# Split weights in slots 3, 5 and 7 of the first expert mixture, and later rank and list steps in its slots

## The chip, the cores and the metric

The kernel runs on one core of one Trainium2 chip. The metric is device time in microseconds (us) of one execution, taken as the median of several runs. Where the text speaks of a profile, it is one execution recorded by the hardware profiler: for each engine the start and the duration of every instruction. Engines are named as the profile names them: PE is the TensorE matmul, PEld its weight load, DVE is VectorE, ACT is ScalarE, POOL is GpSimd, SP is SyncE, whose queue issues the large DMAs.

## What is computed

Attention over 2 x 8 heads of 576 positions feeds a mixture of 8 experts (capacity 288 tokens each), and its output feeds a second mixture of 8 experts. The change lies in the first mixture:

```python
h = np.maximum(np.einsum('ecd,edf->ecf', disp, w1), 0.0)
y = np.einsum('ecf,efd->ecd', h, w2)
for i in range(N):
    if keep[i]:
        out[i] = gate_w[i] * y[expert_idx[i], pos[i]]
```

Here `disp` holds the tokens of an expert (512 features), `w1` is 512 x 1024 and `w2` 1024 x 512 for each expert, all in 32-bit floats. There are 1152 tokens for 8 experts, so an expert has about 144.

## The kernel before

The kernel works in stages: attention (to 108 us in the profile), eight slots of the first mixture (112 to 269 us), five slots of the second (from 269 us). A slot is one expert with a fixed number of token columns. The widths of slots 0 to 7 are 160, 192, 136, 152, 132, 160, 144 and 168; the fullest experts go to the wide ones.

A slot has eight steps (j = 0 to 7), one for each piece of 1024 weight columns, 512 KB. Steps 0 to 3 form the hidden layer from the tokens `xs`, steps 4 to 7 the output `yT` from `hidden`. Each step makes eight products, one weight block of 128 x 128 times all token columns of the slot, so a slot makes 64 products.

There are two ways to make a product (`product`, L848). A native slot multiplies the 32-bit floats directly (L853): the trace shows two matmul records for each product, each with a weight load. A halved slot splits weights and tokens into a head (`hi`, rounded to a shorter mantissa) and a rest (`lo`), and makes two matmuls: the head of the weight times heads and rests of the tokens side by side (L857, twice the columns), and the rest of the weight times the heads of the tokens (L859, one time the columns). Before the change slot 1 alone is halved (L48).

A halved slot needs more from ACT and DVE. `split` (L747) makes for each half piece a cast on ACT (L757) and a subtraction on DVE (L759), 16 of each in a slot. `prep` (L812) turns the tokens on PE in two halves and writes them by a cast on ACT (L845) and a subtraction on DVE (L846), where a native slot has one copy on ACT (L841). `fold` and `fold2` (L902, L921) empty PSUM by an extra copy on ACT and an addition on DVE, and write `hidden` as head and rest.

The order of the work is written by hand on a clock of the kernel's own: `step` (L865) adds the estimated time of each product. `stream` (L1116) asks for piece i of a slot seven steps ahead (`tf`, L1127), and cuts it five steps ahead (`ts`, L1128), so that the pieces 0 to 4 of a halved slot are cut in steps 3 to 7 of the slot before it, and pieces 5 to 7 in its own steps 0 to 2. Piece buffers (`st`) number eight. A native slot gives a buffer back when PE has used it, a halved slot when the piece is split. SP issues the fetches (L142) in a fixed order, among them each slot's write of its result rows (L1013), and reads a register for the second mixture (L1052) that `choose` (L1223) writes in slot 6. Each slot's tail (`tail1`, L947) runs beside the next slot: the second mixture's gate, the rank matmuls (L984 to L987) at `k.T[3]` and the list matmuls (L1016) at `k.T[4]` or `k.T[6]` on the kernel's clock. `T` asks for ranks at 5.6 and lists at 13.0 or 9.9, `TH` at 6.6, 14.2 and 10.9; slot 0 has `TH`, slots 1 to 6 have `T`, slot 7 has `TL`. The tokens of the next slot are turned from step 6 on (L1206), the second half 2.0 later on that clock.

PE's order is pinned. On ACT and DVE the build chooses an order within the given constraints, and each engine then works through its instructions in that order.

```python
clock[0] += k.c / 600 + 0.005 if k.native else \
    k.c / 800 + 0.005 + (k.c / 10000 + 0.021 if 2 * k.c <= 512 else 0.0)
```

Of the kernel before, what the change touches and what calls it, by code (L numbers as in the profile page):

```python
# [16 lines left out]
N, DM, E, F = 1152, 512, 8, 1024  # L17
# [25 lines left out]
T = 1.5, 2.3, 3.0, 5.6, 9.9, 2.0, 13.0  # L43
TL = 0.9, 1.7, 2.4, 4.6, 9.4, 2.0, 13.0
AWAKE = 15, 6, 14, 4
DW = 128 + 2 * E
MID, PLACE = 32, 1.2
HALVED = 1,  # L48
TH = 1.5, 2.3, 3.0, 6.6, 10.9, 2.0, 14.2
BRISK = 1.2  # L50

# [37 lines left out]
def build(tc, ctx, spots, tab, qk, v, s, wg, wa, cap, mod, wg2, mb, wb, out):  # L89
# [687 lines left out]
    def gather(k, idx, xc=None, rows=None):  # L777
        k.xc = xc or rings[k.m][turn[k.m] % 3]
        turn[k.m] += not xc
        k.idx = idx  # L780
        src, rw = (x1, RW) if k.m == 1 else (y1[0:rows or E * C1, :], RW2)
        for i, (_, r) in enumerate(k.rows):
            nc.gpsimd.indirect_dma_start(  # L783
                out=k.xc[:r, i, 0:rw], out_offset=None, in_=src,
                in_offset=bass.IndirectOffsetOnAxis(ap=idx[:r, i:i + 1], axis=0),
                bounds_check=src.shape[0] - 1, oob_is_err=False)
# [7 lines left out]
    def begin(g):  # L794

        agenda.append([clock[0], clock[0], g])
# [15 lines left out]
    def prep(k, after=None):  # L812
        c = k.c
        k.xs = mp.tile([P, 4, c], F32, tag="xs", name="xn", bufs=1) if k.native else \
            mp.tile([P, 4, 2, c], F32R, name="xs", bufs=1)
        per = 2 if 2 * c <= 512 else 1

        def turn_rows(pt, kp, i):
            r0, r = k.rows[i]
            for kk in range(per):  # L820
                kt = kp + kk
                pin(nc.tensor.transpose(pt[:, kk, r0:r0 + r], k.xc[:r, i, kt * P:(kt + 1) * P], ident[:r, :r]))

        ready = {}
        if after is None and per == 2:
            for i in range(len(k.rows)):
                for kp in (0, 2):
                    if not i:
                        ready[kp] = pt_.tile([P, per, c], F32, tag="t", name="ptx")
                    turn_rows(ready[kp], kp, i)  # L830
        for kp in range(0, 4, per):
            if kp:
                yield (1.0 * kp if after else 0.0)
            pt = ready.get(kp)
            if pt is None:
                pt = pt_.tile([P, per, c], F32, tag="t", name="ptx")
                for i in range(len(k.rows)):
                    turn_rows(pt, kp, i)
            with tc.issue_after(after.relu) if after else ExitStack():
                if k.native:  # L840
                    ins = nc.scalar.copy(k.xs[:, kp:kp + per], pt)  # L841
                    fence(ins)
                    continue
                hi = k.xs[:, kp:kp + per, 0, :]
                ins = nc.scalar.copy(hi, pt)  # L845
            fence(ins, nc.vector.tensor_tensor(k.xs[:, kp:kp + per, 1, :], pt, hi.bitcast(F32), op=ALU.subtract))  # L846
# [208 lines left out]
    def pick(m, lst, cv, n=None):  # L1055
        idx = mp.tile([HC[m], W[m]], I32, name="idx", bufs=4)
        src = lst[:, bass.ds(cv, W[m])]
        if n is None:
            nc.gpsimd.tensor_copy(idx, src)
        else:  # L1060
            nc.gpsimd.tensor_tensor(idx, src, hole[:, n, :], op=ALU.add)
        return idx
# [19 lines left out]
    def slot(m, width=None, halved=False):  # L1082
        k = Slot()
        k.m, k.c, k.two = m, width or C[m], True
        k.native = (m == 1 or k.c == H2) and not halved
        k.rows = [(r, min(HC[m], k.c - r)) for r in range(0, k.c, HC[m])]
        k.ranked = k.placed = k.listed = lambda: None
        k.early, k.T, k.last, k.hold, k.next = False, T, False, None, None
        return k
# [20 lines left out]
    def at(n, j, f):  # L1110
        steps.setdefault(8 * n + j, []).append((8 * n + j - 1, f))
# [4 lines left out]
    def stream(n, k, src, known, pace=0.5, late=()):  # L1116

        k.w, k.st = {}, {}

        def get(i):  # L1120
            with tc.issue_after(k.hold()) if k.hold else ExitStack():
                k.st[i] = first[i] if n == 0 and i < len(first) else fetch(src, k.e, i)

        def cut(i):
            k.w[i] = k.st.pop(i) if k.native else split(k.st.pop(i), i, alone=n < E or i in late)
        for i in range(8):
            tf = max(8 * n + i - FETCH, known + pace * i)  # L1127
            ts = 8 * n + i - 2 if i in late else max(8 * n + i - SPLIT, tf + (2 if n < E else 3))  # L1128
            when(tf, lambda i=i: get(i))
            when(ts, lambda i=i: cut(i))  # L1130
# [55 lines left out]
    def know(k, e):  # L1186
        k.e, k.cv = where(1, perm, e - 1)

    for e in range(E):
        k = slot(1, WID[e], e in HALVED)  # L1190
        if seq:
            seq[-1].next = k
        k.early = e not in (E - 3, E - 1)
        k.T = TL if e == E - 1 else TH if e + 1 in HALVED else T
        k.e = e
        k.tail = lambda k=k, e=e: tail1(k, e)
        stream(e, k, wa, never)
        if e:
            steps.setdefault(8 * e - 8, []).append((never, lambda k=k, e=e: know(k, e)))
            at(e - 1, 1, lambda k=k, e=e: gather(k, pick(1, list1, k.cv, n=e)))  # L1200
        else:
            gather(k, list0)
            tc.keep_in_program_order(nc.gpsimd.tensor_copy(hole, con["hole"][:H1]))
            tc.keep_in_program_order(nc.gpsimd.memset(run, 0.0))
            k.idx = pick(1, list1, 0, n=0)
        at(max(e - 1, 0), 6 if e else 0, lambda k=k, e=e: begin(prep(k, after=seq[e - 1])) if e else list(prep(k)))  # L1206
        seq.append(k)
# [116 lines left out]
    for i in range(5):  # L1324
        n = E + i
        k = slot(2, H2 if i == 4 else C2)
# [97 lines left out]
```

## Time and profile before

| | us |
|---|---|
| median of 3 runs | 406.28 |
| lowest and highest of them | 405.71, 406.42 |
| the profiled execution | 402.02 |
| its span, first to last instruction | 400.2 |
| PE busy in the span | 385.4 |

The profiled execution is a run of its own, 4.3 us below the median. Its span leaves 1.8 us around it. Busy time counts an engine as busy while an instruction runs on it; what ended an idle time stands in brackets in the timeline rows. The granted clock is the share of TensorE's full clock; it is 0.996 over the span.

### The profile page before, as it was taken

To read this page: it belongs to the slowest core of one execution; us is meant where nothing else is said; L and a number is where in the kernel's file an instruction comes from. 1 tells how busy PE (TensorE), PEld (TensorE's weight loads), DVE (VectorE), ACT (ScalarE), POOL (GpSimd) and SP (SyncE) were. 2 spreads that over 40 slices of the span, in tenths; PEclk is the share of its full clock that TensorE was granted. 3 is DMA by queue.
4 is the path that set the end of the run, shared out by engine and by line. 5 is a ranking of instruction groups with operands and counts; after the bars stand their busy time and mean duration, and the time that the engine had idled before them with its cause. 6 is when DMAs were issued, how large, how long until landed. Compare 5 with 4: busy or idle time off the path is not lost. (4 is left out here: it accounts for less than half of the span.)

```text
span 400.2 us, 8788 instructions
## 1 busy us (share of the span) xinstructions
PE 385.4 (96%) x3144; PEld 358.1 (89%) x3144; DVE 194.8 (49%) x781; ACT 179.6 (45%) x471; POOL 133.4 (33%) x177
## 2 busy tenths in 40 slices
PE   6899999999999999999999999999999999999991
PEld 3688888898689899999999999999999999999981
DVE  7977778887726853241415051559822342221100
ACT  7999999986325722121212121245423464131220
POOL 5776977550273311210102004000437266030031
PEclk9999999999999999999999999999999999999998
DMA  5864798702159942978797678971169557010020
GB/s 184 276 197 155 262 380 331 269 3 88 50 150 329 379 136 63 322 203 303 226 310 251 236 224 273 275 253 50 42 165 383 167 160 217 12 34 26 2 55 22
DMA packets 30626, 74.66 MB, mean 187 GB/s; under 512 B 9234, under 2 KB 11666, under 8 KB 30572
## 3 DMA queue, kind: packets, MB, share of 16 engines
q1 hardware_dynamic: 24120, 66.73, 49.7%
q0 software_dynamic: 6368, 7.22, 6.8%
q8 instruction: 27, 0.44, 0.5%
q14 instruction: 27, 0.22, 0.2%
q10 hardware_dynamic: 84, 0.04, 0.0%
HBM read 63.78 MB, written 10.51 MB: 186 GB/s over the span
## 5 line engine op out<-in xcount | busy, mean ns | idle before, releaser
L853 PE MATMUL ps<-xn,st 128*128 128x160 f32 (+6 forms) x512 | 70.4, 290 | 0.4 <-ACT xn L841 0.4
L853 PEld LDWEIGHTS ps<-xn,st 128*128 128x128 f32 x512 | 66.2, 190 | 0.6 <-ACT xn L841 0.6
L853 PE MATMUL ps<-hidden,st 128*128 128x160 f32 (+5 forms) x448 | 62.9, 294 | 0.0
L853 PEld LDWEIGHTS ps<-hidden,st 128*128 128x128 f32 x448 | 58.5, 190 | 0.5
L482 ACT ACTIVATE e<-sc,nmx 128x192 f32<-128x192 f32 (+4 forms) x80 | 44.7, 561 | 3.0 <-DVE sc L478 2.4
L919 DVE COPY yT<-ps 128x276 f32<-128x276 f32 (+6 forms) x22 | 8.0, 362 | 69.2 <-ACT yT L918 69.2
L861 PE MATMUL ps<-xs,hi 128*128 128x276 f32 x128 | 38.4, 300 | 0.0
L861 PE MATMUL ps<-hidden,hi 128*128 128x276 f32 x128 | 38.1, 298 | 0.0
L862 PE MATMUL ps<-xs,hi 128*128 128x276 f32 x128 | 37.1, 290 | 0.0
L863 PE MATMUL ps<-xs,lo 128*128 128x276 f32 x128 | 37.1, 290 | 0.0
L863 PE MATMUL ps<-hidden,lo 128*128 128x276 f32 x128 | 37.1, 290 | 0.0
L862 PE MATMUL ps<-hidden,hi 128*128 128x276 f32 x128 | 37.0, 289 | 0.0
L783 POOL DMA_INDIRECT xc<-x,idx x14 | 15.1, 1078 | 63.2 <-DVE eq L976 46.6
L394 PE MATMUL pt<-ident,e 128*128 128x128 f32 x240 | 34.7, 275 | 0.8 <-ACT eT L498 0.7
L918 ACT COPY yT<-ps 128x276 f32<-128x276 f32 (+6 forms) x22 | 7.1, 323 | 58.6 <-PE ps L853 31.2
L478 DVE TENSOR_SCALAR_CACHE_REDUCE sc<-ps 128x192 f32<-128x192 f32 (+4 forms) x80 | 31.6, 417 | 2.3 <-ACT e L482 0.8
L394 PE MATMUL ps<-ka,qa 128*128 128x320 f32 (+2 forms) x96 | 29.9, 326 | 2.0 <-DVE qa L358 1.3
L759 DVE TENSOR_TENSOR lo<-st,hi 128x512 fp32r<-128x512 f32 x40 | 27.4, 707 | 5.8 <-ACT hi L757 5.7
L1023 POOL DMA_INDIRECT out<-yr,oi x12 | 14.4, 1201 | 45.6 <-ACT yr L940 43.2
L757 ACT CAST hi<-st 128x512 fp32r<-128x512 f32 x48 | 27.6, 619 | 4.5 <-DMA st<-in_wa 4.5
L394 PEld LDWEIGHTS pt<-ident,e 128*128 128x128 f32 x240 | 26.2, 141 | 1.8 <-ACT eT L498 0.9
L932 DVE SCALAR_TENSOR_TENSOR hidden<-ps,hidden 128x552 fp32r<-128x552 f32 x16 | 11.7, 732 | 30.0 <-ACT hidden L930 29.9
(301 smaller groups left out, 854.2 us busy)
## 6 DMA issues: line engine op xcount, KB each, us to landing
st<-in_wa SPq DMA_DIRECT2D x64, 512.0 KB, 5.6
st<-in_wb SPq DMA_DIRECT2D x24, 512.0 KB, 6.4
qkd<-in_qk SPq DMA_DIRECT2D x6, 1152.0 KB, 5.4
y<-yr SPq DMA_DIRECT2D x8, 390.0 KB, 3.8
vt<-in_v SPq DMA_DIRECT2D x8, 320.0 KB
qkd<-in_qk SPq DMA_DIRECT2D x4, 576.0 KB, 4.9
out<-zrow SPq DMA_DIRECT2D x1, 2304.0 KB
x<-xrow SPq DMA_DIRECT2D x2, 768.0 KB
```

Of the source, the lines that this page charges most:

```text
L394: ins = op(*args, **kw)
L478: least[:] = [nc.vector.tensor_scalar(h.sc[t][:r, c0:c1], ps[:r, o0:o0 + c1 - c0], -0.125, low, op0=ALU.mult, op1=ALU.min, accum_out=h.nmx ...
L482: recent[:] = [nc.scalar.activation(ebuf[t, i][:r, :w], h.sc[t][:r, :w], AF.Exp, bias=h.nmx[t][:r], scale=-1.0, accum_out=rsum[:r, k.b, t, ...
L757: nc.scalar.copy(hi[:, c:c + h], st[:, c:c + h])
L759: eng.tensor_tensor(lo[:, c:c + h], st[:, c:c + h], hi[:, c:c + h].bitcast(F32), op=ALU.subtract)
L783: nc.gpsimd.indirect_dma_start(out=k.xc[:r, i, 0:rw], out_offset=None, in_=src, in_offset=bass.IndirectOffsetOnAxis(ap=idx[:r, i:i + 1], a ...
L853: pin(nc.tensor.matmul(out[:, 0:c], w[:, o:o + P], mv, start=first, stop=last, skip_group_check=True))
L861: pin(nc.tensor.matmul(out[:, 0:c], hi, mv[:, 0, :], start=first, stop=False, skip_group_check=True))
L862: pin(nc.tensor.matmul(out[:, 0:c], hi, mv[:, 1, :], start=False, stop=False, skip_group_check=True))
L863: pin(nc.tensor.matmul(out[:, 0:c], lo, mv[:, 0, :], start=False, stop=last, skip_group_check=True))
L932: fence(relu, nc.vector.scalar_tensor_tensor(k.hs[:, 2 * j:2 * j + 2, 1, :], k.b, 0.0, hi.bitcast(F32), op0=ALU.max, op1=ALU.subtract))
L1023: put = nc.gpsimd.indirect_dma_start(out=out, out_offset=bass.IndirectOffsetOnAxis(ap=oi[:, i:i + 1], axis=0), in_=yr[:, i, :], in_offset= ...
```

## The change

The tuple of halved slots grows from slot 1 to slots 1, 3, 5 and 7, and slots 1 to 6 take the later set of times `TH`.

```diff
-HALVED = 1,
+HALVED = 1, 3, 5, 7
 TH = 1.5, 2.3, 3.0, 6.6, 10.9, 2.0, 14.2
...
-        k.T = TL if e == E - 1 else TH if e + 1 in HALVED else T
+        k.T = TL if e == E - 1 else TH
```

By it, slots 3, 5 and 7 (152, 160 and 168 columns) multiply split heads and rests. Slot 7 keeps `TL`.

## Rows read from the trace of the kernel before

**Rows 1.** The page, busy us, share of the span and instructions.
```profile
PE 385.4 (96%) x3144; PEld 358.1 (89%) x3144; DVE 194.8 (49%) x781; ACT 179.6 (45%) x471; POOL 133.4 (33%) x177
```
**Rows 2.** Busy by stretch, slots 0, 1, 3, 5, 7: length; PE, PEld, DVE, ACT, POOL; clock; DMA.
```profile
112.58:130.69 18.11, 18.11 (x137) 18.11 (x137) 8.59 (x17) 8.01 (x18) 8.79 (x15) 1.00 0.84 271
130.69:152.79 22.10, 21.73 (x163) 20.75 (x162) 12.74 (x43) 9.86 (x21) 4.96 (x5) 1.00 0.61 222
170.95:190.71 19.76, 19.76 (x163) 19.01 (x161) 6.01 (x32) 3.88 (x11) 2.15 (x3) 1.00 0.80 260
208.40:228.99 20.59, 20.59 (x162) 19.78 (x161) 6.20 (x32) 3.97 (x11) 2.19 (x3) 1.00 0.75 245
247.41:268.64 21.23, 21.23 (x166) 20.72 (x165) 10.22 (x39) 6.68 (x17) 0.50 (x1) 1.00 0.86 252
```
**Rows 3.** Timeline of PE, native runs: start, length, engine, line, operation, columns, records.
```profile
181.03 4.30 PE L853 MATMUL ps<-hidden,st 128*128 128x152 f32 x32
218.90 4.51 PE L853 MATMUL ps<-hidden,st 128*128 128x160 f32 x32
258.35 2.44 PE L853 MATMUL ps<-hidden,st 128*128 128x168 f32 x16
383.46 1.70 PE L853 MATMUL ps<-xn,st 128*128 128x92 f32 x14
```
**Rows 4.** Timeline of PE and PEld, slot 1 (halved) and a slot of 276 columns.
```profile
142.26 0.36 PE L857 MATMUL ps<-hidden,hi 128*128 128x384 f32 x1
...
146.56 0.36 PE L857 MATMUL ps<-hidden,hi 128*128 128x384 f32 x1
...
131.26 0.19 PEld L857 LDWEIGHTS ps<-xs,hi 128*128 128x128 f32 x1
131.37 0.19 PEld L859 LDWEIGHTS ps<-xs,lo 128*128 128x128 f32 x1
...
367.86 0.29 PE L861 MATMUL ps<-hidden,hi 128*128 128x276 f32 x1
...
369.90 0.29 PE L862 MATMUL ps<-hidden,hi 128*128 128x276 f32 x1
```
**Rows 5.** Timeline of PE, the rank matmul in slot 1; idle time before it in brackets.
```profile
139.75 0.21 PE L984 MATMUL pr<-oh,upper 96*96 96x16 bf16 x1 [0.37 <-DVE oh L981]
```
**Rows 6.** Timeline of ACT and DVE, end of slot 0, before the halved slot 1.
```profile
124.31 1.14 ACT L757 CAST hi<-st 128x512 fp32r<-128x512 f32 x2 [1.29 <-DMA st<-in_wa]
126.86 1.14 ACT L757 CAST hi<-st 128x512 fp32r<-128x512 f32 x2 [0.64 <-DMA st<-in_wa]
128.27 1.14 ACT L757 CAST hi<-st 128x512 fp32r<-128x512 f32 x2
129.31 0.48 ACT L845 CAST xs<-ptx 128x384 fp32r<-128x384 f32 x1
129.19 1.28 DVE L759 TENSOR_TENSOR lo<-st,hi 128x512 fp32r<-128x512 f32 x2
130.39 0.55 DVE L846 TENSOR_TENSOR xs<-ptx,xs 128x384 fp32r<-128x384 f32 x1
```
**Rows 7.** Timeline of SP: third pieces of slots 3, 5, 7, and a fourth piece.
```profile
160.26 0.33 SPq L142 DMA_DIRECT2D st<-in_wa  x1
198.02 0.33 SPq L142 DMA_DIRECT2D st<-in_wa  x1
236.92 0.34 SPq L142 DMA_DIRECT2D st<-in_wa  x1
240.23 0.33 SPq L142 DMA_DIRECT2D st<-in_wa  x1
```
**Rows 8.** Line L142, issue to landing in us, slot 2, then slot 4.
```profile
DMA to landing us min/median/max: 5.5/5.5/5.5
DMA to landing us min/median/max: 6.0/6.0/6.0
```
**Rows 9.** Waits of SP's queue in slot 6: us in total, times, longest.
```profile
SPq L1052 <- DVE sres L1235: 1.7, 1, 1.7
```

## The prediction

> **What bounds the kernel now.** I read the page first: PE is busy for 385.4 of 400.2 us, while DVE and ACT stand below half [rows 1]. Then the stretches by slot: in the native slots 3, 5 and 7 PE is busy for the whole stretch at a granted clock of 1.00, the higher level of 2.4 GHz; slot 1, the halved one, has 0.37 us in which PE is idle [rows 2]. So in these slots the end is set by what PE has to stream, and whatever PE is made to wait for is added in full. A saving on PE counts only while DVE, ACT and the fetches keep up. That is why I then read the price of a product in either form, and after that what surrounds the start of the one halved slot.
>
> **Price of a native product.** 32 records in a run of 4.30 us at 152 columns, less the 0.30 that the last one takes by itself, stand 129.0 ns apart. At 160 columns it is 135.8 ns, at 168 columns 142.0 ns [rows 3]. Two records make a product: 258, 272 and 284 ns.
>
> **Price of a halved product.** At 192 columns fifteen products go by between 142.26 and 146.56, so one costs 286.7 ns [rows 4]. I need it at 152 to 168 columns, which the trace of before doesn't show. Two rows say how it is made up. The load of the head and the load of the rest that follows it start 110 ns apart, 131.26 and 131.37 [rows 4], and native passes of only 92 columns also stand 110 ns apart ((1.70 - 0.27)/13) [rows 3]. So I take 110 ns as the least time between two matmuls that each need a new block of weights. The rest's matmul at 192 columns needs less than that by its columns, so it costs 110 ns, and the head's matmul (384 columns) has what is left, 177 ns or 0.461 ns a column. In a slot of 276 columns sixteen matmuls from 367.86 to 369.90 stand 127.5 ns apart [rows 4], 0.462 ns a column: the same rate. With that, a product costs 110 + 0.461 x 2c: 250 ns at 152 columns, 257.5 at 160, 265 at 168. The saving is 7.9, 14.1 and 19.1 ns a product, 41.1 ns in all, times 64 products: **2.6 us**. It is small because only the head's matmul gets cheaper with fewer columns. The bounds are 2.0 and 3.2 us, from 3 ns a product either way, the difference between the two readings of the rate plus the rounding of the rows.
>
> The Trainium skill, page "TensorE: Matmul & The Clock Gate", section "Back-to-back issue gap", gives about 81 ns for a matmul of 128 columns with its load, less than the 110 taken here. By it the rest's matmul would cost about 25 ns less a product, some 4.8 us more saving in all by an estimate from that page. The 92-column passes at 110 ns speak against it.
>
> **What the halved form adds on PE.** Slot 1 lasts 22.10 us; less 64 x 0.2867 and the 0.37 of waiting, 3.38 us are left for transposes, gate, ranks and lists. Slot 5 has 20.59 - 64 x 0.2716 = 3.21 us for the same [rows 2 to 4]. So 0.17 us a slot, **0.5 us** for three.
>
> **The rank wait.** In slot 1 PE waits 0.37 us for the one-hots of the tail [rows 5], because DVE has the last splits between the steps of that chain. In slots 3, 5 and 7 the chain has the same work beside it; by the kernel's clock the ranks come after 27 to 29 products instead of 24, at 250 to 265 ns instead of 287, so some 0.3 us later in real time. That nearly closes the gap. I take **0.2 us** for three slots; the bounds are 0 and 1.1 (three times 0.37). Asking later for ranks and lists in the other slots costs PE nothing: the same matmuls are made, only a few products later, and the lists are still within the slot. What waits for a list is the gather for slot 8, whose tokens are turned only near the end of slot 7.
>
> **The start of the halved slots.** This is the term that decides. At the end of slot 0 ACT and DVE work in the order in which the code asks: split of piece 2 (124.31), copy of `yT`, split of piece 3, first half of `xs`, split of piece 4, second half of `xs`, whose subtraction ends at 130.39 + 0.55 = 130.94. ACT stood idle for the landing of piece 2 (1.29 us) and of piece 3 (0.64 us) [rows 6]: work behind a piece that isn't there waits with it. From the landing of piece 2 to the second half of `xs` it is 130.94 - 124.31 = 6.6 us, of which 0.64 us is the wait for piece 3; so 6.0 to 6.6 us. Slot 1 started at 130.69 [rows 2] and needed that half for its third product, two products or 0.57 us later: there were 0.3 us to spare.
>
> In slots 2, 4 and 6 piece 2 of the next slot is issued later against the slot's end, since the write of result rows stands in the same queue and the rows of a gather come at the same time. It is issued at 160.26, 198.02 and 236.92 [rows 7]; landing takes 5.5 us in slot 2 and 6.0 in slot 4 [rows 8], and I take 5.75 in slot 6. It is there at 165.8, 204.0 and 242.7. Adding 6.0 to 6.6, the second half of `xs` is written at 171.8 to 172.4, 210.0 to 210.6 and 248.7 to 249.3. PE wants it two products (0.5 us) after the starts at 170.95, 208.40 and 247.41 [rows 2]: 171.45, 208.9, 247.9. So PE waits 0.35 to 0.95, 1.1 to 1.7 and 0.8 to 1.4 us, together 2.3 to 4.0 us; I take **3.1 us**. While the slots were native their `xs` was one copy on ACT with no split ahead of it, so nothing of this wait exists now. What follows it is not late: the splits that come next have their pieces, and the rank chain moves with the slot.
>
> **Other edits.** 24 more pieces are split, 48 casts and 48 subtractions (0.57 and 0.64 us each in pairs [rows 6]), some 10 us of ACT and DVE a slot. DVE is busy for 6.0 of 19.8 us in slot 3 and for 12.7 of 22.1 in slot 1 [rows 2], so the room is there apart from the slots' starts. Buffers come back earlier, which pulls the native slot's fetches ahead, as after slot 1 now; the bytes don't change. I cost both at nothing; if that cover were gone, each further piece landing late would cost up to the 1.29 us seen on ACT [rows 6].
>
> **Sum.** -2.6 + 0.5 + 0.2 + 3.1 = +1.2 us: 402.0 becomes 403.2 in the profiled execution, and on the median 406.28 + 1.2 = **407.5 us**. From the bounds: -3.2 + 0.5 + 0 + 2.3 = -0.4 to -2.0 + 0.5 + 1.1 + 4.0 = +3.6, so 405.9 to 409.9 for this case alone.
>
> **Rivals.**
>
> A, faster: the build orders the writes of `xs` ahead of the splits of pieces 3 and 4, so no slot starts late. Then -2.6 + 0.5 + 0.2 = -1.9 us, 404.4. For it: the tokens are turned well before the slot ends, and nothing forces the split first. Against it: at the end of slot 0 both engines took the splits first [rows 6].
>
> B, faster: the products are as cheap as the kernel's own clock says (L867): 231, 242 and 253 ns. Then the saving is 26.8 + 29.6 + 31.2 = 87.6 ns times 64 = 5.6 us, and the sum is -1.8 us, 404.5. For it: the formula gives 285 ns at 192 columns, which fits. Against it: at 152 columns it leaves less than 110 ns for the second matmul beside the 140 of the first. The page named above leans to this side.
>
> C, much slower: in slot 6 SP reads a register that `choose` writes, and holds the fetch of piece 3 behind it until 240.23 [rows 7, 9]. With ranks four products later (1.0 us) and the two subtractions of a piece ahead (1.28 us [rows 6]), that fetch goes out at 242.5 and lands at 248.0. From piece 3 to the second half of `xs` it was 130.94 - 126.86 = 4.1 us, so 252.1 against 247.9 wanted: 4.2 us in place of 1.1. That makes +4.3 us, 410.6. It decides as soon as piece 3 lands later than 1.9 us after piece 2. Against it: the fetch may be put ahead of the read.
>
> **How the numbers follow.** My forecast has 0.50, A 0.20, B 0.10, C 0.12, and 0.08 is left for what I don't see. A measurement of this kernel tells about 0.2%, 0.8 us, from no change. Of the forecast's 0.50 most lies above that bound, 0.33, with 0.15 within it and 0.02 below. A gives 0.18 faster and 0.02 same, B 0.07, 0.02 and 0.01, C is slower, the rest 0.04, 0.02, 0.02. Sums: faster 0.31, same 0.21, slower 0.48. The range reaches from A and B with the better end of the saving (403.6) to the upper end of the forecast (409.9); C and the tails are left out.
>
> **What would show it.** Right: runs of halved products at 250, 257 and 265 ns; PE idle for 0.4 to 1.7 us at the third product of slots 3, 5 and 7, ended by DVE's `xs` subtraction; ACT idle for DMA in slots 2, 4 and 6. Wrong: slots 3, 5 and 7 shorter by over 0.5 us with PE never idle at their start (A), products near 231 ns (B), or an idle time over 3 us in slot 7 alone (C). If PE's waits let the granted clock fall to its lower level, all of it would be too low; in the 0.37 us of slot 1 it stayed at 1.00 [rows 2, 5].

## The result, and the profile after

The kernel with slots 3, 5 and 7 halved takes 410.78 us (409.16 to 411.64), the kernel before 405.69 us (403.23 to 406.42) beside it. The ratio on record is 1.0147, interval 1.0116 to 1.0177: slower, by some 6 us, or by 5.1 us if the two medians are subtracted. Of 1.2 us forecast, the sign was right; the predicted time was 407.5 us, and 410.78 lies above the upper end of 409.9.

The page of the kernel after; columns as in [rows 1].

```profile
PE 386.2 (94%) x3144; PEld 357.5 (87%) x3144; DVE 230.2 (56%) x847; ACT 211.0 (52%) x531; POOL 137.2 (33%) x177
```

PE is busy for 0.8 us more than before, and the span is 9.4 us longer (409.6 against 400.2): nearly all of the time went into PE standing still. 2.6 of the 9.4 us lie ahead of slot 0, which starts at 115.20 instead of 112.58. Nothing was changed there. Slot 0 starts at 115.2 in two of the experiments' traces too, and at 112.4 to 113.0 in the other nine, halved slots or not; so I leave the 2.6 us out, and why they come and go stays open. The rest is read slot by slot.

Busy by stretch in the kernel after: slots 2 to 7 in order, then three parts of slot 6. Columns as in [rows 2], with GB/s last.

```profile
155.41:174.22 18.81, 18.36 (x163) 17.37 (x161) 11.16 (x42) 8.77 (x21) 3.87 (x5) 1.00 0.75 239
174.22:194.35 20.13, 19.28 (x160) 18.43 (x161) 12.65 (x45) 9.32 (x22) 3.49 (x3) 1.00 0.75 264
194.35:212.60 18.25, 17.85 (x162) 16.97 (x160) 11.23 (x42) 8.64 (x21) 2.11 (x3) 1.00 0.74 243
212.60:233.31 20.71, 19.85 (x160) 18.96 (x161) 12.86 (x45) 9.63 (x23) 3.61 (x3) 1.00 0.73 262
233.31:256.94 23.63, 20.25 (x163) 19.62 (x161) 14.10 (x55) 9.31 (x21) 4.88 (x5) 0.93 0.72 235
256.94:277.27 20.33, 20.00 (x168) 19.51 (x166) 15.54 (x49) 12.15 (x27) 0.00 (x0) 1.00 0.67 210
...
246.40:249.70 3.30, 0.00 (x0) 0.00 (x0) 2.66 (x12) 1.13 (x2) 0.00 (x0) 1.00 0.98 364
249.86:253.27 3.41, 3.41 (x17) 3.40 (x18) 1.19 (x3) 1.41 (x4) 1.59 (x3) 0.50 0.91 311
253.30:256.90 3.60, 3.60 (x32) 3.60 (x32) 2.81 (x6) 1.69 (x4) 2.51 (x2) 1.00 0.79 239
```

Before, slots 2 to 7 took 18.16, 19.76, 17.69, 20.59, 18.42 and 21.23 us (the three odd ones in [rows 2]). So slot 2 is longer by 0.65 us, slot 3 by 0.37, slot 4 by 0.56, slot 5 by 0.12 and slot 6 by 5.21, and slot 7 is shorter by 0.90: together 6.0 us. Another 0.8 us lie in the second mixture, in this one execution; I didn't follow them. Slots 0 and 1 are as before. Slot 6 in the kernel before, columns as in [rows 2]:

```profile
228.99:247.41 18.42, 18.42 (x163) 18.01 (x162) 6.84 (x43) 3.97 (x11) 3.61 (x5) 1.00 0.76 241
```

The native slot 6 carries nearly all of it. In it PE does nothing for 3.30 us and more. From 249.86 to 253.27 the granted clock is 0.50, the lower level of 1.2 GHz: 17 records in 3.41 us, while right behind it 32 go by in 3.60 us at 1.00. The timeline of PE in the kernel after shows what it waited for there and elsewhere.

```profile
174.22 0.41 PE L857 MATMUL ps<-xs,hi 128*128 128x304 f32 x1 [0.45 <-DVE xs L846]
175.80 0.41 PE L857 MATMUL ps<-xs,hi 128*128 128x304 f32 x1 [0.85 <-DVE xs L846]
...
212.60 0.41 PE L857 MATMUL ps<-xs,hi 128*128 128x320 f32 x1 [0.40 <-DVE xs L846]
214.20 0.41 PE L857 MATMUL ps<-xs,hi 128*128 128x320 f32 x1 [0.86 <-DVE xs L846]
214.53 0.34 PE L857 MATMUL ps<-xs,hi 128*128 128x320 f32 x1
214.79 0.35 PE L857 MATMUL ps<-xs,hi 128*128 128x320 f32 x1
...
249.76 0.53 PE L1016 MATMUL plist<-colm,pos 96*92 96x144 f32 x2 [3.38 <-DVE colm L191]
...
266.16 0.17 PE L984 MATMUL pr<-oh,upper 96*96 96x16 bf16 x1 [0.33 <-DVE oh L981]
```

The waits for tokens (`xs`) at the starts of slots 3 and 5 are there, 2.56 us in all: 0.85 and 0.86 us for the second half, which I had forecast, and 0.45 and 0.40 us for the first half, which I had not. The one of 3.38 us I had not forecast: the list matmul of slot 5's tail, in the middle of slot 6, waits for `colm`, which DVE writes. Here is why DVE was late, by its own timeline and ACT's in slot 6 of the kernel after.

```profile
240.11 0.62 ACT L757 CAST hi<-st 128x512 fp32r<-128x512 f32 x1 [0.71 <-DMA st<-in_wa]
243.22 0.62 ACT L757 CAST hi<-st 128x512 fp32r<-128x512 f32 x1 [1.36 <-DMA st<-in_wa]
246.39 1.14 ACT L757 CAST hi<-st 128x512 fp32r<-128x512 f32 x2 [1.85 <-DMA st<-in_wa]
...
241.91 0.16 DVE L989 TENSOR_TENSOR run<-run,pr 128x8 f32<-128x8 f32 x1 [0.21 <-PE pr L987]
241.99 0.69 DVE L759 TENSOR_TENSOR lo<-st,hi 128x512 fp32r<-128x512 f32 x1
...
243.87 0.69 DVE L759 TENSOR_TENSOR lo<-st,hi 128x512 fp32r<-128x512 f32 x1 [1.05 <-ACT hi L757]
244.92 0.15 DVE L997 TENSOR_REDUCE rank<-dd 96x2 f32<-96x16 f32 x1
...
245.22 0.68 DVE L759 TENSOR_TENSOR lo<-st,hi 128x512 fp32r<-128x512 f32 x1
247.04 0.69 DVE L759 TENSOR_TENSOR lo<-st,hi 128x512 fp32r<-128x512 f32 x1 [0.87 <-ACT hi L757]
...
247.97 0.68 DVE L759 TENSOR_TENSOR lo<-st,hi 128x512 fp32r<-128x512 f32 x1
...
249.26 0.45 DVE L191 TENSOR_TENSOR colm<-ctab,hj 96x288 fp32r<-96x288 f32 x1
```

Read it upwards from the last line. From the rank sums (`run`, 241.91) to the start of `colm` it is 7.35 us. The small steps between, most of them 0.14 to 0.23 us long, have five subtractions of slot 7's split among them in DVE's order. Before two of the five DVE stands idle for a cast, 1.05 and 0.87 us; these casts had stood at the head of ACT's queue until their pieces landed, with ACT idle for 1.36 and 1.85 us. (The 0.71 us lie ahead of `run`.) In the kernel before, slot 7 was native, nothing was split in slot 6, and the same steps took 2.75 us.

```profile
236.57 0.16 DVE L989 TENSOR_TENSOR run<-run,pr 128x8 f32<-128x8 f32 x1 [0.86 <-PE pr L987]
...
239.32 0.45 DVE L191 TENSOR_TENSOR colm<-ctab,hj 96x288 fp32r<-96x288 f32 x1
```

(The timeline of DVE in slot 6 of the kernel before.) So two things lengthen the chain. The five subtractions take up some 0.6 us each, 3.0 us; the waits for casts add 1.92 us; 2.4 us are the chain's own steps. By an estimate from these figures PE would still have waited for the list for some 1.5 us of the 3.4 if all pieces had been there. The list of ACT's waits sums it up: casts that wait for a landing, us in total, times, longest; the kernel before, then after.

```profile
ACT hi L757 <- DMA st<-in_wa: 4.5, 4, 1.5
```

```profile
ACT hi L757 <- DMA st<-in_wa: 21.1, 13, 4.0
```

### The profile page after: what moved, and what is told of

It reads as the page before. It is cut to its first block, busy times and chain, and to the rows that moved or that the text cites. A ratio compares the mean times of both kernels' runs of the same rounds, so it can differ in the third digit from the quotient of the medians.

```text
span 409.6 us, 8909 instructions
## 1 busy us (share of the span) xinstructions
PE 386.2 (94%) x3144; PEld 357.5 (87%) x3144; DVE 230.2 (56%) x847; ACT 211.0 (52%) x531; POOL 137.2 (33%) x177
## 4 chain that ended last, share of the span: by engine, by line
PE 69%; DMA 12%; issue 7%; DVE 7%; ACT 3%; POOLq 0%; POOL 0%; SPq 0%; ACTq 0%
PE ps L853 10%; PE ps L857 10%; PE ps L861 6%; PE ps L862 6%; PE ps L863 6%; PE ps L394 6%; PE pt L394 6%; DMA st<-in_wa 4%; PE ps L859 4%; DMA qkd<-in_qk 3%; PE pb L394 3%; PE pty L939 3%; DVE lo L759 2%; PE ptx L822 2%; PE px L394 2%
## 5 line engine op out<-in xcount | busy, mean ns | idle before, releaser
L759 DVE TENSOR_TENSOR lo<-st,hi 128x512 fp32r<-128x512 f32 x88 | 59.2, 692 | 16.9 <-ACT hi L757 16.7
L757 ACT CAST hi<-st 128x512 fp32r<-128x512 f32 x96 | 56.0, 618 | 21.1 <-DMA st<-in_wa 21.1
L853 PE MATMUL ps<-xn,st 128*128 128x160 f32 (+4 forms) x320 | 41.8, 284 | 0.4 <-ACT xn L841 0.4
L853 PEld LDWEIGHTS ps<-xn,st 128*128 128x128 f32 x320 | 39.6, 190 | 0.6 <-ACT xn L841 0.6
L857 PE MATMUL ps<-xs,hi 128*128 128x384 f32 (+3 forms) x128 | 37.1, 360 | 2.6 <-DVE xs L846 2.6
L857 PE MATMUL ps<-hidden,hi 128*128 128x384 f32 (+3 forms) x128 | 36.2, 356 | 0.0
L853 PE MATMUL ps<-hidden,st 128*128 128x160 f32 (+3 forms) x256 | 35.4, 294 | 0.0
L853 PEld LDWEIGHTS ps<-hidden,st 128*128 128x128 f32 x256 | 33.3, 196 | 0.3
L859 PE MATMUL ps<-xs,lo 128*128 128x192 f32 (+3 forms) x128 | 30.8, 241 | 0.0
L859 PE MATMUL ps<-hidden,lo 128*128 128x192 f32 (+3 forms) x128 | 30.8, 240 | 0.0
```

Source lines behind the costliest of these rows:

```text
L757: nc.scalar.copy(hi[:, c:c + h], st[:, c:c + h])
L759: eng.tensor_tensor(lo[:, c:c + h], st[:, c:c + h], hi[:, c:c + h].bitcast(F32), op=ALU.subtract)
L853: pin(nc.tensor.matmul(out[:, 0:c], w[:, o:o + P], mv, start=first, stop=last, skip_group_check=True))
L857: pin(nc.tensor.matmul(out[:, 0:2 * c], hi, mv.rearrange("p s c -> p (s c)"), start=first, stop=False, skip_group_check=True))
L859: pin(nc.tensor.matmul(out[:, c:2 * c], lo, mv[:, 0, :], start=False, stop=last, skip_group_check=True))
```

## The experiments

Theory after the result: neither part of the change costs the whole of it alone. Slot 7's splits, asked for while their pieces are still on the way, hold up the chain from ranks to lists on DVE, and the later times put that chain among them. Rivals: the later times alone do it; or it is the register of the second mixture (C). No kernel leaves anything out of the computation. Times are medians, 402.52 to 402.75 us for the kernel before beside them; the ratio to it carries its interval. The kernel after was not run again beside them, so it is compared by its ratio, 1.0147.

| kernel | us | ratio | interval |
|---|---|---|---|
| later times alone | 402.74 | 0.9997 | 0.9982 to 1.0011 |
| halved slots alone, old times | 404.15 | 1.0039 | 1.0013 to 1.0064 |
| without slot 7 | 403.50 | 1.0032 | 0.9997 to 1.0067 |
| slot 7 without 3 and 5 | 407.26 | 1.0103 | 1.0064 to 1.0141 |
| list of slot 5 asked later still | 407.37 | 1.0111 | 1.0052 to 1.0170 |
| pieces 3 and 4 cut a step later | 406.27 | 1.0061 | 1.0032 to 1.0090 |
| all pieces cut a step later | 400.86 | 0.9954 | 0.9930 to 0.9978 |
| the same, without slot 7 | 401.11 | 0.9967 | 0.9940 to 0.9995 |
| the same, slot 1 alone halved | 402.63 | 0.9994 | 0.9965 to 1.0024 |
| cut later, old times | 399.80 | 0.9917 | 0.9888 to 0.9946 |
| cut later, gather for slot 8 first | 399.88 | 0.9919 | 0.9889 to 0.9949 |

Every trace is of one execution. Three of them were well above the median of their kernel: 406.22 us with halved slots alone, 409.38 with pieces 3 and 4 later, 401.11 with the gather first. A wait read there may be shorter, or absent, in the other executions.

The diffs are against the kernel after.

### One part at a time

```diff
-HALVED = 1, 3, 5, 7
+HALVED = 1,
```

> Only slot 1 is halved, as before the change, but slots 1 to 6 have the later times TH. My theory: later ranks and lists cost nothing by themselves; they cost only where splits stand on VectorE between the rank and the list. So the time is that of the kernel before, 405.7 us, within 0.8 us, and slot 6 lasts 18.4 us as before. Rival (the later request itself makes the list in slot 6 wait): slot 6 is at least 2 us longer and the time at least 407.7 us.

The ratio is 0.9997, and slot 6 lasts 18.42 us as before. The later times alone cost nothing.

```diff
-        k.T = TL if e == E - 1 else TH
+        k.T = TL if e == E - 1 else TH if e + 1 in HALVED else T
```

> Slots 1, 3, 5 and 7 are halved, but slots 1, 3 and 5 keep the earlier times T, so in slot 6 the ranks come 4 products (1 us) and the list 4 products earlier than in the changed kernel. My theory: the list's one-hots stand behind the splits of pieces 0 to 2 whose fetches land late, so the list still waits; between 2 and 4.5 us of idle PE in slot 6 and 409 to 411.5 us. Rival (the later request is the cause): the rank chain gets past the splits, no wait above 0.5 us in slot 6, and at most 407 us.

The list's wait fell to 0.31 us, against the 2 to 4.5 us that I expected of my theory; here the rival was right. The ranks come 1.0 earlier on the kernel's clock, `run` is written at 237.66 and `colm` is begun at 241.60, 3.94 us later, with two subtractions of the split in between instead of five and no wait for a cast above 0.2 us. The traced execution still loses: 1.71 us by waits for the second half of the tokens in slots 3 and 5, and more at another place, PE in slot 7, and the clock behind it.

```profile
263.86 0.30 PE L822 MATMUL ptx<-ident,yc 92*128 92x92 f32 x1 [2.05 <-DMA yc<-y,idx]
```

```profile
265.20:268.40 3.20, 3.20 (x18) 3.20 (x16) 1.43 (x5) 1.14 (x3) 0.00 (x0) 0.50 0.07 27
```

PE waits for the gather of slot 8's tokens. Its landing takes 11.0 to 13.2 us, before 7.5 to 8.8 (issue to landing of the three parts):

```profile
DMA to landing us min/median/max: 11.0/12.4/13.2
```

```profile
DMA to landing us min/median/max: 7.5/8.2/8.8
```

The first line is of this kernel, the second of the kernel before. A halved slot 7 gives its piece buffers back when they are split, so the weights of slot 8 are fetched beside the gather: from 248.60 to 263.80 the DMA share is 1.03, at 318 GB/s. The median run loses 1.6 us, this execution 3.7; how long the gather took in the others isn't known.

### With slot 7 and without it

```diff
-HALVED = 1, 3, 5, 7
+HALVED = 1, 3, 5
```

> Slots 1, 3 and 5 are halved, slot 7 is native, TH stays. My theory: no splits in slot 6, so its list doesn't wait and the clock doesn't fall: slot 6 is back at 18.4 us. Slots 2 to 5 keep what they lost, 0.65 + 0.37 + 0.56 + 0.12 = 1.7 us by the two traces, so 405.7 + 1.7 = 407.4 us. Rival (the loss is spread over the fetches of all slots): above 409 us.

By the ratio 1.3 us are lost, near the 1.7 expected, but the interval reaches down to 0.9997, so the times alone don't show a loss. In the trace slots 2 to 5 are longer by 1.1 us together. Slot 6 is normal (18.45 us, clock 1.00). The starts of slots 3 and 5 wait for the second half of the tokens as in the kernel after; the waits for the first half (0.45 and 0.40 us there) are absent.

```profile
173.24 0.41 PE L857 MATMUL ps<-xs,hi 128*128 128x304 f32 x1 [0.86 <-DVE xs L846]
...
211.34 0.41 PE L857 MATMUL ps<-xs,hi 128*128 128x320 f32 x1 [0.86 <-DVE xs L846]
```

```diff
-HALVED = 1, 3, 5, 7
+HALVED = 1, 7
```

> Slots 1 and 7 halved, TH as in the change. My theory: nothing is lost in slots 2 to 5, and the whole loss of slots 6 and 7 is here: the list's wait of 3.4 us, 1.7 us of slower clock, less about 1 us that slot 7 gains: ratio 1.008 to 1.013. Rival (the list waits because the halved slots before it have shifted the fetches): below 1.004.

Slot 6 lasts 23.52 us, with the same wait and the same clock behind it. So the loss in slot 6 comes with slot 7's halved form and the later times, whatever slots 3 and 5 do.

```profile
245.54 0.39 PE L1016 MATMUL plist<-colm,pos 96*92 96x144 f32 x2 [3.31 <-DVE colm L191]
```

```profile
246.10:249.40 3.30, 3.30 (x17) 3.29 (x17) 1.82 (x5) 2.17 (x6) 2.08 (x3) 0.50 0.82 272
```

### Asking later still for the list

```diff
-        k.T = TL if e == E - 1 else TH
+        k.T = TL if e == E - 1 else TH[:4] + (14.2,) + TH[5:] if e == E - 3 else TH
```

> The changed kernel, but the list of slot 5 is asked for in slot 6 at 14.2 on the kernel's clock in place of 10.9, some 13 products later. My theory: the one-hots are written by then, PE doesn't wait, the clock stays at 2.4 GHz, and 5.1 us come back; of these 0.5 to 1 us go to a wait for the second half of the tokens at the start of slot 7, so 406 to 407 us. Rival (the engines behind are overloaded, the wait only moves to the start of slot 7 or to slot 8's gather): at least 409 us.

The list's wait is gone and the clock stays at 1.00; slot 6 lasts 18.46 us. But slot 7 lasts 23.13 us, and the ratio, 1.0111, is far above what I expected of my theory. The rival had it: the wait moves on, to the tokens of slot 7 and to a gather that is now issued late, at 253.56.

```profile
253.10 0.43 PE L857 MATMUL ps<-xs,hi 128*128 128x336 f32 x1 [1.07 <-DVE xs L846]
...
266.77 0.55 PE L822 MATMUL ptx<-ident,yc 92*128 92x92 f32 x2 [1.10 <-DMA yc<-y,idx]
```

### Cutting the pieces later

If the cause is that a split reaches the head of ACT's queue ahead of its data, asking for it one step later should take all these waits away at once.

```diff
-            ts = ... max(8 * n + i - SPLIT, tf + (2 if n < E else 3))
+            ts = ... max(8 * n + i - SPLIT, tf + 3)
```

> The changed kernel with one number moved: a piece is split four steps ahead of its use in place of five. My theory: what makes the waits is splits that stand at the head of ACT's and VectorE's queues before their piece has landed. One step later the pieces are there, so the waits for the tokens at the starts of slots 3 and 5 (0.45 + 0.85 and 0.40 + 0.86 us) and the list's wait in slot 6 (3.4 us and 1.7 us of slower clock) are gone; slots 3, 5 and 7 keep their savings of 0.5, 0.7 and up to 1.2 us. Ratio to the kernel before 0.993 to 0.998. Rival (the two engines have too much to do around these slots, whatever the order): the waits move to the rank matmuls of the halved slots, ratio above 1.003.

That is what happens: 0.9954, faster than before. ACT's waits for landings fall from 21.1 to 1.9 us. `colm` is begun at 239.55, 2.95 us after `run` and not 7.35, with one subtraction of the split between them and the others behind. The list doesn't wait, and the clock stays at 1.00 from 140 to 290 us. Of the waits for tokens 0.16 us is left, in slot 5. The timeline of DVE in slot 6, then of ACT in slot 2, in this kernel:

```profile
236.60 0.16 DVE L989 TENSOR_TENSOR run<-run,pr 128x8 f32<-128x8 f32 x1 [0.21 <-PE pr L987]
...
236.77 0.68 DVE L759 TENSOR_TENSOR lo<-st,hi 128x512 fp32r<-128x512 f32 x1
...
239.55 0.45 DVE L191 TENSOR_TENSOR colm<-ctab,hj 96x288 fp32r<-96x288 f32 x1
239.92 1.88 DVE L759 TENSOR_TENSOR lo<-st,hi 128x512 fp32r<-128x512 f32 x3
```

```profile
166.98 1.14 ACT L757 CAST hi<-st 128x512 fp32r<-128x512 f32 x2 [0.51 <-DMA st<-in_wa]
```

The step count fits this. A piece is asked for seven steps ahead and cut five ahead, two steps later. In slot 6 two of eight steps are 18.42 x 2/8 = 4.6 us, and a landing takes 5.5 to 6.0 us [rows 8]; three steps are 6.9 us (an estimate: steps are not all of one length). What this edit doesn't part is the waiting from the work: it lets the pieces land, and it also moves four of the five subtractions out of the chain.

```diff
-            ts = ... max(8 * n + i - SPLIT, tf + (2 if n < E else 3))
+            ts = ... max(8 * n + i - SPLIT, tf + (3 if n >= E or i in (3, 4) else 2))
```

> The changed kernel, but only pieces 3 and 4 of a slot are split one step later; pieces 0 to 2 stay five steps ahead. My theory: the second half of the tokens no longer stands behind three pieces, so the waits at the starts of slots 3 and 5 go (2.6 us), while the list in slot 6, which stands behind pieces 0 to 2, still waits over 2 us: ratio 1.006 to 1.010. Rival (one cause for all): below 1.003.

The ratio is 1.0061, at the lower edge of what I expected. The list's wait (3.4 us) remains, and slot 6 lasts 23.63 us as in the kernel after: that comes from pieces 0 to 2. Slot 3's wait for tokens is gone, but slot 5's is still there in the trace, 0.22 and 0.85 us, and there the expectation missed. So pieces 3 and 4 are not all of what the tokens stand behind.

```profile
212.69 0.41 PE L857 MATMUL ps<-xs,hi 128*128 128x320 f32 x1 [0.85 <-DVE xs L846]
```

The next two cut all pieces later, with the line for `ts` as in the first edit of this section. One is without slot 7, one has slot 1 alone halved and the old times, which makes it the kernel before with later splits.

```diff
-HALVED = 1, 3, 5, 7
+HALVED = 1, 3, 5
```

> Slots 1, 3 and 5 halved, slot 7 native, splits four steps ahead. My theory: no waits are left, slots 3 and 5 save 0.5 and 0.7 us: ratio 0.995 to 0.999, some 1.2 us faster than before. Rival (halving these narrow slots saves nothing in the end): 1.000 or above.

```diff
-HALVED = 1, 3, 5, 7
+HALVED = 1,
...
-        k.T = TL if e == E - 1 else TH
+        k.T = TL if e == E - 1 else TH if e + 1 in HALVED else T
```

> The kernel before (slot 1 alone halved, T and TH as there) with splits four steps ahead in place of five. My theory: slot 1 had no wait at its start, so there is nothing to win: ratio 0.998 to 1.002, and the gain of the kernel that splits four steps ahead in slots 1, 3, 5 and 7 comes from the halved slots. Rival (splitting later is the gain by itself): below 0.997.

Without slot 7 it is 0.9967, and slots 3 and 5 are shorter than before by 0.52 and 0.93 us. With slot 1 alone it is 0.9994: cutting later wins nothing by itself, the gain comes from the halved slots.

### Two ways to clear what is left

With all pieces cut later, PE still waits 0.63 us for slot 8's gather:

```profile
260.17 0.30 PE L822 MATMUL ptx<-ident,yc 92*128 92x92 f32 x1 [0.63 <-DMA yc<-y,idx]
```

One way is to ask earlier for ranks and lists in the native slots, as the kernel before did; the other is to hold slot 8's fetches until its gather has landed (they are asked for later on the kernel's clock too).

```diff
-            ts = ... max(8 * n + i - SPLIT, tf + (2 if n < E else 3))
+            ts = ... max(8 * n + i - SPLIT, tf + 3)
...
-        k.T = TL if e == E - 1 else TH
+        k.T = TL if e == E - 1 else TH if e + 1 in HALVED else T
```

> Slots 1, 3, 5 and 7 halved, splits four steps ahead, but slots 1, 3 and 5 with the earlier times T. My theory: with no split ahead of the rank chain the later times do neither good nor harm on PE; the list of slot 6 and the gather for slot 8 come 1 us earlier, which shortens the 0.6 us wait for that gather in slot 7: ratio 0.993 to 0.997. Rival (the halved slots need the later times): above 0.998.

```diff
-            ts = ... max(8 * n + i - SPLIT, tf + (2 if n < E else 3))
+            ts = ... max(8 * n + i - SPLIT, tf + 3)
...
+        info["first"] = nc.sync.dma_start(landed, seq[E].xc[0:1, :, 0]).ins
...
-            if i:
-                k.hold = lambda: info["landed"]
+            k.hold = (lambda: info["landed"]) if i else (lambda: info["first"])
...
-            ... stream(n, k, wb, 8 * (E - 2) + 4, late=range(8))
+            ... stream(n, k, wb, 8 * (E - 1) + 1, late=range(8))
```

> As the kernel with splits four steps ahead, but the fetches for slot 8 wait until the gather for slot 8 has landed. My theory: that gather is late in slot 7 because the halved slot gives its buffers back early and the fetches for slot 8 are moved at the same time; held back, the wait of 0.6 us in slot 7 goes, and slot 7 lasts 20.5 us or less: ratio 0.991 to 0.996. Rival (the gather is late because its list is late): the 0.6 us stay.

Both take the wait away, and they can't be told apart (0.9917 and 0.9919). The first did better than the 0.993 to 0.997 that I expected. Both beat the kernel before, and by their ratios the kernel after; their intervals overlap that of the later cut alone (0.9930 to 0.9978) at its lower end. Slots 3, 5 and 7 of the first one (cut later, old times), columns as in [rows 2]:

```profile
170.71:189.95 19.24, 19.24 (x164) 18.42 (x162) 12.19 (x44) 10.21 (x23) 3.49 (x3) 1.00 0.80 289
...
207.60:227.25 19.65, 19.65 (x163) 18.94 (x162) 12.40 (x45) 10.36 (x23) 3.60 (x3) 1.00 0.79 282
...
245.61:265.94 20.33, 20.00 (x167) 19.51 (x166) 16.37 (x51) 13.19 (x29) 0.55 (x1) 1.00 0.89 301
```

PE is busy for the whole of slots 3 and 5 again, and in slot 7 idle for 0.33 us only, the wait for the one-hots. In the profile of the other one, PE waits 0.85 us for the tokens of slot 5; that execution took 1.2 us more than the median, so the wait may be its own. Why there and not here stays open, as does slot 5's wait with pieces 3 and 4 cut later. The two edits together were not tried.

## Why the prediction went wrong, step by step

**Price of a product: right.** In the kernel after, a product costs 251 ns at 152 columns, 259 at 160 and 266 at 168 (medians from one start to the next), forecast 250, 257.5 and 265. In slot 5 two starts stand 0.26 us apart, 214.53 and 214.79 above. Rival B's 231 to 253 ns are out. The saving is then 7 + 12.6 + 18 = 37.6 ns, times 64, 2.4 us for the 2.6 forecast.

The Trainium skill, page "TensorE: Matmul & The Clock Gate", section "Back-to-back issue gap", gives about 81 ns for a 128-column matmul with its load. The measured products side with the 110 ns taken from this kernel's own rows.

**What the halved form adds on PE: too high.** I took 0.5 us from slot 1. With the waits out of the way, slot 3 has 19.24 - 64 x 0.251 = 3.18 us beside its products, and as a native slot it had 19.76 - 64 x 0.258 = 3.25. There is nothing to add. The net gain of the three slots without any forecast wait is 0.52 + 0.94 + 0.90 + 0.33 = 2.7 us, where I had 2.1.

**The rank wait: right.** 0.33 us in slot 7, none in slots 3 and 5; I took 0.2, with bounds of 0 and 1.1.

**The start of the halved slots: right in mechanism, near in size in part by luck.** Slot 3 waits 1.30 us (forecast 0.35 to 0.95), slot 5 1.26 us (1.1 to 1.7). In slot 7 there is none; slot 6 had been made so long that the tokens were ready. With the list asked later still slot 6 has its usual length, and the wait is there, 1.07 us. Together it is 2.56 us for 3.1. In slot 3 two errors met, in opposite directions. Piece 2 was issued 9.07 us after the start of slot 2 (at 164.48), before 7.47: the result rows stand ahead of it in SP's queue, and their write waited 2.4 us for a step of the tail on DVE (the reciprocal at 163.59), before 0.6. That step came right behind a subtraction for which DVE had waited 1.12 us, so the splits also held up a fetch. From its landing at 170.4 to the second half of `xs` at 175.75 it was 5.35 us, not 6.0 to 6.6.

**"Asking later for ranks and lists in the other slots costs PE nothing", and the extra splits at nothing: this step failed.** By the first experiment it holds with one halved slot. With slot 7 halved it doesn't: in slot 6 it cost a wait of 3.38 us and 1.8 us of slower clock behind it, where the sum had 0. I counted PE's matmuls, saw that they were the same, and took the rest from "the room is there apart from the slots' starts". That room was DVE's busy share, 0.3 of a slot. I never followed the chain between the ranks and the list through DVE's queue, though I had named the same thing for `xs`: work behind a piece that isn't there waits with it. In slot 6, pieces 0 to 2 of slot 7 are in DVE's and ACT's queues too, and the later times move the chain in among them: five subtractions in place of two. Their own 3.0 us count for more in the chain than the 1.92 us of waiting for casts. The row that should have sent me there was in my hands: [rows 6] shows 1.29 us of ACT idle for one piece, and I gave it as the price of each further piece only "if that cover were gone", without asking which chain stood behind.

**"What follows is not late": this failed with it.** The lists are late in slot 6; with the old times, the gather is late in slot 7.

**The clock: named, not counted.** I wrote that the sum would be too low if waits let the granted clock fall. It fell behind the 3.38 us. Slot 6 is longer by 5.21 us; the wait is 3.38 of it, so 1.8 us are what came after it. 3.41 us at half the clock do the work of 1.7, so that is the clock.

**The sum** of slots 2 to 7: -2.7 + 0.33 + 2.56 + 3.38 + 1.8 = 5.4 us of the 6.0. The 0.6 us left lie mostly around the waits at the slots' starts: slot 2 is 0.65 us longer with a wait of 0.45, slot 4 0.56 with 0.40, and slot 5 is 0.20 longer without its wait than the same slot of the kernel with cuts later and old times. The record that follows a wait takes 0.41 us, and the next one starts 0.33 us after it and not 0.26 (214.20, 214.53 and 214.79 above).

**Rivals.** A was wrong for the kernel after; its sum, -1.9 us, is near what the later cut gives (-1.8 us with the new times, -3 with the old). C gave nearly the right time, 410.6 us, in nearly the right place, for the wrong reason; that the two times meet is luck. Its held fetch didn't happen: SP reads the register at 248.0, and by then five fetches had gone out from 241.08 on; one alone came behind the read. The timeline of SP in slot 6 of the kernel after, and the read of `sres` (durations in ns, first and last start):

```profile
241.08 0.33 SPq L142 DMA_DIRECT2D st<-in_wa  x1
242.70 0.91 SPq L142 DMA_DIRECT2D st<-in_wa  x2
245.93 0.91 SPq L142 DMA_DIRECT2D st<-in_wa  x2
248.76 0.33 SPq L142 DMA_DIRECT2D st<-in_wa  x1
```

```profile
L1052 SPq TENSOR_LOAD <-sres x1: 278/278/278, 248.0 to 248.0; - x1
```

A time that fits is no proof of its mechanism.

## What to carry to other kernels

When an edit puts work that waits for a DMA into an engine's queue, follow every other chain through that queue until the next landing, the tail of the stage before too, and count in that chain both the wait and the work itself; a low busy share says nothing about what stands at the head. Ask for such work late enough that its data has landed: here one step later turned a loss of 6 us into a gain of about 2, and with the earlier ranks 3. A wait on PE can cost more than its length: here 3.38 us of waiting took another 1.8 us by the clock.

## What the runs showed of the hardware

- An idle time of PE of 3.38 us (3.31 with slots 1 and 7 halved) is followed by a granted clock of 0.50, the level of 1.2 GHz, for about 3.4 us. With the old times alone the idle time is 2.05 us; PE then works for 1.2 us at 1.00, and from 265.20 to 268.40 the clock is 0.50. Idle times of 1.07 and 1.10 us left it at 1.00 (list asked later still).
- The same gather lands in 7.5 to 8.8 us before, at a DMA share of 0.94 (243.5 to 255.5 us), and in 11.0 to 13.2 us with the old times alone, at a share of 1.03. With slot 8's fetches held back the share is 0.63 (244 to 256 us), and all three parts are there 9.5 us after the first was issued.
